# A full rewrite of a block-sparse attention plus Hyena-gate kernel: fp16 gate, wide exps, natural-layout PV, radix-2 DFT, merged work streams

## The chip, the cores and the metric

The kernel runs on one core of one Trainium2 chip. The metric is the time of one execution in device microseconds. Each kernel was run several times, in rounds that alternate with the kernel before on the same chip, and one execution was recorded by the hardware profiler (its span is a microsecond or two shorter than the time). A run that is over 1.5% above the fastest run of the same kernel is called slow and is left out of ratios. The engines are PE (matrix multiplication), PEld (PE's weight loads, which overlap its matmuls), DVE (vector engine), ACT (scalar engine), POOL and SP (which only issues transfers here). PSUM is the memory that PE's results go to; a program divides it into buffers.

## The reference, cut to what matters

```python
def _attn_ref(q, k, v):                       # 4 batches, 8 heads, 768 positions, head size 64
    k_rep = k.reshape(B, H, 12, 64, D).mean(axis=3)           # one mean key per block of 64
    gate_scores = einsum('bhsd,bhnd->bhsn', q, k_rep)         # then causal by blocks
    top_idx = argsort(gate_scores)[..., -3:]                  # the 3 best blocks, and the own block
    scores = scale * q @ k.T                                  # masked by blocks and causally
    return softmax(scores) @ v

def _moe_ref(x, w_proj, filter_fft, w_out):   # x: 4 x 768 x 512
    x1, x2, x3 = split(x @ w_proj, 3)
    x2_conv = irfft(rfft(x2) * rfft(filter_fft))              # along the 768 positions
    return (x1 * x2_conv * x3) @ w_out
```

## The kernel before: the parts that matter here

Attention runs head by head. Scores are computed transposed (keys on partitions) in pieces of 128 to 384 queries, each with its own exp. PV (the product of the exps with V) is also transposed: the stationary operand is V with 64 columns of ones beside it, so rows 64 to 127 of the result hold the softmax sum, 64 times over. Its reciprocal is made on ACT from a logarithm and an exponential.

```python
    ps_sc = ... bufs=3      # scores, and much else
    ps_ot = ... bufs=1      # the PV sum: one buffer
    ...
                    nc.tensor.matmul(sps, lhsT=augK[...], rhs=augQ[0:76, qs:qe], ...)
                    nc.scalar.activation(ex[:, 0:w], sps, AF.Exp, bias=bias_exp, scale=scale)
                    ...                                   # POOL: causal mask on diagonal pieces
                    nc.tensor.matmul(oT[:, qs - hs:qe - hs], lhsT=v_aug[:, kc, :], rhs=ex[:, 0:w], ...)
            # once per half of a head, 64 times in all:
            nc.scalar.activation(den[64:128, :], oT[64:128, :], AF.Ln, bias=0.0, scale=1.0)
            nc.scalar.activation(den[64:128, :], den[64:128, :], AF.Exp, bias=0.0, scale=-1.0)
            nc.vector.tensor_tensor(out=xT[...], in0=oT[0:64, :], in1=den[64:128, :], op=ALU.mult)
```

The gate is an fp32 matmul with the queries as the stationary operand and only 12 moving columns. The FFT of the Hyena part is a full real DFT by matmul: 2 x 3 groups of six 512-column matmuls forward, and six of 384 columns for each piece of the inverse. Hyena of a batch is added as low-priority pieces during the attention of the next batch.

The softmax here doesn't subtract the row's maximum and nothing guards it: scores larger than these inputs give would overflow.

Of the kernel before, what the change touches and what calls it, by code (L numbers as in the profile page):

```python
# [9 lines left out]
FP32 = mybir.dt.float32  # L11
# [7 lines left out]
def kernel(  # L19
# [10 lines left out]
    nc = tc.nc  # L30
# [3 lines left out]
    SC = S // P  # L34
    NBLK = S // 64
    Dm = H * D
    DC = Dm // P
    N3 = 3 * Dm
    F = 384
    FCH = S // P  # L40
    HALF = 384

    scale = 1.0 / math.sqrt(D)
    GBIG = 240.0
    EXPB = -GBIG * scale
    CBIG = 1.0e5
    BIG2 = 1.0e9
    TWO_PI = 2.0 * math.pi
    MAGIC = float(2 ** 23)

    fp = FP16

    const = ctx.enter_context(tc.tile_pool(name="const", bufs=1))
    hpool = ctx.enter_context(tc.tile_pool(name="hpool", bufs=3))
    aug = ctx.enter_context(tc.tile_pool(name="aug", bufs=5))
    augp = ctx.enter_context(tc.tile_pool(name="augp", bufs=5))
    qtfp = ctx.enter_context(tc.tile_pool(name="qtfp", bufs=3))
    expp = ctx.enter_context(tc.tile_pool(name="expp", bufs=8))
    small = ctx.enter_context(tc.tile_pool(name="small", bufs=6))
    xtp = ctx.enter_context(tc.tile_pool(name="xtp", bufs=2))  # L60
    p2 = ctx.enter_context(tc.tile_pool(name="p2", bufs=1))
    p2b = ctx.enter_context(tc.tile_pool(name="p2b", bufs=2))
    outp = ctx.enter_context(tc.tile_pool(name="outp", bufs=3))

    ps_trans = ctx.enter_context(tc.tile_pool(name="ps_trans", bufs=1, space=bass.MemoryType.PSUM))
    ps_sc = ctx.enter_context(tc.tile_pool(name="ps_sc", bufs=3, space=bass.MemoryType.PSUM))
    ps_ot = ctx.enter_context(tc.tile_pool(name="ps_ot", bufs=1, space=bass.MemoryType.PSUM))
    ps_ms = ctx.enter_context(tc.tile_pool(name="ps_ms", bufs=2, space=bass.MemoryType.PSUM))

    def tr_tile(name, shape, dtype=FP32):  # L70
        return ps_trans.tile(list(shape), dtype, name=name, tag="trans", padded_shape=[P, 1024])

    def sc_tile(name, shape=(P, 512), dtype=FP32):
        return ps_sc.tile(list(shape), dtype, name=name, tag="sc")

    def ot_tile(name, shape=(P, HALF), dtype=FP32):
        return ps_ot.tile(list(shape), dtype, name=name, tag="ot")

    def ms_tile(name, shape=(P, 512), dtype=FP32):
        return ps_ms.tile(list(shape), dtype, name=name, tag="ms")  # L80

    id_f32 = const.tile([P, P], FP32)
    make_identity(nc, id_f32)
    id_f16 = const.tile([P, P], fp)
    nc.gpsimd.tensor_copy(id_f16, id_f32)

    ebig = const.tile([P, S], fp)
    nc.gpsimd.memset(ebig[64:76, :], GBIG)
    nc.gpsimd.affine_select(
        out=ebig[64:76, :], in_=ebig[64:76, :], compare_op=ALU.is_ge,  # L90
        fill=0.0, base=0, pattern=[[1, S]], channel_multiplier=-64)
    nc.gpsimd.affine_select(
        out=ebig[64:76, :], in_=ebig[64:76, :], compare_op=ALU.is_ge,
        fill=0.0, base=63, pattern=[[-1, S]], channel_multiplier=64)

    ownb = const.tile([P, SC, NBLK], fp)
    nc.gpsimd.memset(ownb, 0.0)
    nc.gpsimd.affine_select(
        out=ownb[0:64], in_=ownb[0:64], compare_op=ALU.not_equal,
        fill=1.0, base=0, pattern=[[-2, SC], [1, NBLK]], channel_multiplier=0)  # L100
    nc.gpsimd.affine_select(
        out=ownb[64:128], in_=ownb[64:128], compare_op=ALU.not_equal,
        fill=1.0, base=-1, pattern=[[-2, SC], [1, NBLK]], channel_multiplier=0)

    eavg = const.tile([P, SC, NBLK], FP32)
    nc.gpsimd.memset(eavg, 0.0)
    nc.gpsimd.affine_select(
        out=eavg[0:64], in_=eavg[0:64], compare_op=ALU.not_equal,
        fill=1.0 / 64.0, base=0, pattern=[[-2, SC], [1, NBLK]], channel_multiplier=0)
    nc.gpsimd.affine_select(  # L110
        out=eavg[64:128], in_=eavg[64:128], compare_op=ALU.not_equal,
        fill=1.0 / 64.0, base=-1, pattern=[[-2, SC], [1, NBLK]], channel_multiplier=0)
    NW = P + NBLK
    ideav = const.tile([P, SC, NW], FP32)
    for c in range(SC):
        nc.gpsimd.tensor_copy(ideav[:, c, 0:P], id_f32)
        nc.gpsimd.tensor_copy(ideav[:, c, P:NW], eavg[:, c, :])

    e01f = const.tile([P, S], FP32)
    nc.gpsimd.memset(e01f[64:76, :], 1.0)  # L120
    nc.gpsimd.affine_select(
        out=e01f[64:76, :], in_=e01f[64:76, :], compare_op=ALU.is_ge,
        fill=0.0, base=0, pattern=[[1, S]], channel_multiplier=-64)
    nc.gpsimd.affine_select(
        out=e01f[64:76, :], in_=e01f[64:76, :], compare_op=ALU.is_ge,
        fill=0.0, base=63, pattern=[[-1, S]], channel_multiplier=64)
    cmat = const.tile([P, NBLK], FP32)
    nc.gpsimd.memset(cmat[64:76, :], 0.0)
    nc.gpsimd.affine_select(
        out=cmat[64:76, :], in_=cmat[64:76, :], compare_op=ALU.is_ge,  # L130
        fill=-CBIG, base=0, pattern=[[-1, NBLK]], channel_multiplier=1)

    tri01 = const.tile([P, P], fp)
    nc.gpsimd.memset(tri01, 1.0)
    nc.gpsimd.affine_select(
        out=tri01, in_=tri01, compare_op=ALU.is_ge,
        fill=0.0, base=0, pattern=[[1, P]], channel_multiplier=-1)

    bias_exp = const.tile([P, 1], FP32)
    nc.gpsimd.memset(bias_exp, EXPB)  # L140
    cr0 = const.tile([P, 1], FP32)
    nc.gpsimd.memset(cr0, 2.0 / S)
    nc.gpsimd.memset(cr0[0:1, :], 1.0 / S)
    cr0n = const.tile([P, 1], FP32)
    nc.gpsimd.memset(cr0n, -2.0 / S)
    nc.gpsimd.memset(cr0n[0:1, :], -1.0 / S)

    tvals = const.tile([1, S], fp)
    nc.gpsimd.iota(tvals, pattern=[[1, S]], base=0, channel_multiplier=0,
                   allow_small_or_imprecise_dtypes=True)  # L150
    fvals = const.tile([1, S], fp)
    nc.gpsimd.iota(fvals, pattern=[[0, 2], [1, F]], base=0, channel_multiplier=0,
                   allow_small_or_imprecise_dtypes=True)
    onesrow = const.tile([1, S], fp)
    nc.gpsimd.memset(onesrow, 1.0)
    offrow = const.tile([1, S], fp)
    nc.gpsimd.memset(offrow[:, 0:F], 192.0)
    nc.gpsimd.memset(offrow[:, F:S], 384.0)
    altrow = const.tile([1, S], fp)
    nc.gpsimd.iota(altrow, pattern=[[0, S // 2], [1, 2]], base=0, channel_multiplier=0,  # L160
                   allow_small_or_imprecise_dtypes=True)
    nc.gpsimd.tensor_scalar(altrow, in0=altrow, scalar1=-2.0, scalar2=1.0, op0=ALU.mult, op1=ALU.add)
    altcol = const.tile([P, 1], fp)
    acp = sc_tile("acp", (P, 1))
    nc.tensor.matmul(acp, lhsT=altrow[:, 0:P], rhs=onesrow[:, 0:1], start=True, stop=True)
    nc.vector.tensor_copy(altcol, acp)

    RT = const.tile([P, FCH, S], fp)
    R = const.tile([P, FCH, S], fp)

    def gen_dft_piece(dst_ap, rvals_ap, cvals_ap, off_ap, ncols):
        pr = sc_tile("dftp", (P, ncols))
        nc.tensor.matmul(pr, lhsT=rvals_ap, rhs=cvals_ap, start=True, stop=False)
        nc.tensor.matmul(pr, lhsT=onesrow[:, 0:P], rhs=off_ap, start=False, stop=True)
        ka = p2b.tile([P, 512], FP32, name="dft_ka", tag="dft_ka")
        nc.vector.tensor_scalar(ka[:, 0:ncols], in0=pr, scalar1=1.0 / S,
                                scalar2=MAGIC, op0=ALU.mult, op1=ALU.add)
        nc.vector.tensor_scalar(ka[:, 0:ncols], in0=ka[:, 0:ncols], scalar1=-MAGIC,
                                scalar2=-float(S), op0=ALU.add, op1=ALU.mult)
        nc.vector.tensor_add(pr, pr, ka[:, 0:ncols])  # L180
        nc.scalar.activation(dst_ap, pr, AF.Sin, bias=0.0, scale=TWO_PI / S)

    for tcn in range(FCH):
        rv = tvals[:, P * tcn:P * (tcn + 1)]
        gen_dft_piece(RT[:, tcn, 0:F], rv, fvals[:, 0:F], offrow[:, 0:F], F)
        gen_dft_piece(RT[:, tcn, F:S], rv, fvals[:, F:S], offrow[:, F:S], F)
    for rc in range(FCH):
        rv = fvals[:, P * rc:P * (rc + 1)]
        offsl = offrow[:, 0:F] if rc < 3 else offrow[:, F:S]
        gen_dft_piece(R[:, rc, 0:F], rv, tvals[:, 0:F], offsl, F)  # L190
        gen_dft_piece(R[:, rc, F:S], rv, tvals[:, F:S], offsl, F)

    wp = const.tile([P, DC, N3], fp)
    wo = const.tile([P, DC, Dm], fp)
    fil = const.tile([P, SC, Dm], fp)
    with tc.tile_pool(name="staging", bufs=2) as staging:
# [51 lines left out]
    def attention_prep(b, h):  # L248
# [45 lines left out]
        for c in range(SC):  # L294
            nc.vector.max(m8[:, c, :], gps[:, c, :])
# [200 lines left out]
```

## Time and profile before

The median is 678.2 us (678.15 to 682.07 in the first three runs).

| | PE | DVE | ACT | POOL |
|---|---|---|---|---|
| busy, us of a span of 684.2 | 510 | 263 | 443 | 135 |
| share | 75% | 38% | 65% | 20% |

The mean granted PE clock is 0.790 of full speed. The first lines below are from the profile page of the kernel before: busy time of each engine in all, and the granted clock in 40 equal slices of the span, in tenths of full speed.

```profile
PE 510.1 (75%) x2467; PEld 301.8 (44%) x2467; DVE 263.1 (38%) x675; ACT 443.3 (65%) x665; POOL 134.5 (20%) x327
PEclk9999766655688886985666888895577868898999
```

The next lines are the groups of instructions on ACT and two of PE (line, engine, operation, output<-input, shapes, count, then busy us and mean ns of one, then idle time before them and who ended it).

```profile
L325 ACT ACTIVATE ex<-sps,bias_exp 128x384 f16<-128x384 f32 x160 | 89.6, 580 | 21.2 <-PE sps L322 18.4
L334 ACT ACT_TABLE_LOAD x64 | 82.1, 1283 | 1.2
L325 ACT ACT_TABLE_LOAD x49 | 62.9, 1283 | 3.2 <-PE sps L322 2.4
L335 ACT ACT_TABLE_LOAD x16 | 20.5, 1283 | 0.3
L289 PE MATMUL gps<-krep,qTf 76*128 76x12 f32 x384 | 63.7, 303 | 1.2 <-DVE t_4507 L384 0.9 <-DVE t_3363 L384 0.3
```

130 table loads, by which ACT changes between functions (129 at these three lines, one more at the start), take 167 us. The Trainium skill, "ScalarE: Activation LUTs", section "What ACT_TABLE_LOAD costs", gives about 1283 ns for one; the trace agrees to the nanosecond. (The same sentence of it adds about 1380 ns of drain to every switch. That doesn't show in this trace: in the lines below, the next activation starts within 0.02 us of the load's end.) The timeline of ACT around 160 us (start, length, what):

```profile
163.21 1.28 ACT L334 ACT_TABLE_LOAD   x1
164.51 0.49 ACT L334 ACTIVATE den<-oT_1293 64x384 f32<-64x384 f32 x1
165.01 1.28 ACT L325 ACT_TABLE_LOAD   x1
166.31 0.58 ACT L325 ACTIVATE ex<-sps,bias_exp 128x384 f16<-128x384 f32 x1
166.91 0.52 ACT L335 ACTIVATE den<-den 64x384 f32<-64x384 f32 x1
```

The view of waits: PE waits for exps that would free a score buffer (engine, line, waited for: us in total, times, longest).

```profile
DVE xT L336 <- ACT den L335: 152.3, 58, 6.3
PE sps L322 <- ACT ex L325: 103.0, 71, 3.4
```

### The profile page before, as it was taken

Reading aid. Unit: us, or ns where it says so; the run is one execution under the profiler, and the core shown is the slowest. Engines: PE = TensorE matmul, PEld = TensorE weight load, DVE = VectorE, ACT = ScalarE, POOL = GpSimd, SP = SyncE. Lnnn points to the kernel's source line nnn. Section 1 sums busy time; section 2 is a strip of 40 time slices with the busy share of each in tenths; the row PEclk is TensorE's granted clock in tenths of the full one; section 3 lists DMA queues with packets and bytes.
Section 4 is the critical chain, followed back from the end, with each engine's and each line's share of the span. In section 5 each row is a group of like instructions: output and inputs, shape, how many; then the busy total and the mean of one; then the engine's idle time right before and its main releaser. Section 6 shows DMA issues by size and latency. Waiting matters only on the chain.

```text
span 684.2 us, 7602 instructions
## 1 busy us (share of the span) xinstructions
PE 510.1 (75%) x2467; PEld 301.8 (44%) x2467; DVE 263.1 (38%) x675; ACT 443.3 (65%) x665; POOL 134.5 (20%) x327
## 2 busy tenths in 40 slices
PE   0547877785788767969948867887966867858987
PEld 0212655562664545536714344444734343433343
DVE  3785323221344334423413333532322434431562
ACT  0134699999987898561199789663179899663302
POOL 9410011212111224110012133220011133200130
PEclk9999766655688886985666888895577868898999
DMA  7541222212323221400312121310210000001002
GB/s 253 142 104 39 58 52 56 53 44 61 74 42 64 57 57 44 106 13 13 93 55 60 43 55 22 71 25 21 67 60 24 7 9 0 1 0 55 38 1 92
DMA packets 88199, 36.46 MB, mean 53 GB/s; under 512 B 80480, under 2 KB 82912, under 8 KB 88160
## 3 DMA queue, kind: packets, MB, share of 16 engines
q1 hardware_dynamic: 84704, 29.69, 18.4%
q10 hardware_dynamic: 3456, 6.29, 2.4%
q8 instruction: 19, 0.31, 0.2%
q14 instruction: 20, 0.16, 0.1%
HBM read 24.64 MB, written 6.29 MB: 45 GB/s over the span
## 4 chain that ended last, share of the span: by engine, by line
PE 44%; ACT 34%; issue 11%; DVE 5%; POOL 4%; DMA 0%; POOLq 0%; SPq 0%; ACTq 0%
ACT ex L325 11%; ACT L334 8%; PE tp L268 6%; PE gps L289 6%; PE cv L398 5%; PE sps L322 4%; ACT den L334 3%; ACT den L335 3%; PE x2ps L355 3%; PE op L424 2%; PE x3p L409 2%; ACT L325 2%; PE x1p L404 2%; ACT L335 2%; ACT augQ L276 2%
## 5 line engine op out<-in xcount | busy, mean ns | idle before, releaser
L325 ACT ACTIVATE ex<-sps,bias_exp 128x384 f16<-128x384 f32 (+2 forms) x288 | 135.1, 508 | 63.6 <-PE sps L322 29.6
L322 PE MATMUL sps<-augQ,augK 76*128 76x384 f16 (+2 forms) x288 | 90.0, 349 | 107.6 <-ACT ex L325 103.0
L327 POOL TENSOR_SCALAR_AFFINE_SELECT ex<-ex 128x128 f16<-128x128 f16 x192 | 55.0, 292 | 439.5 <-ACT ex L325 436.8
L268 PEld LDWEIGHTS tp<-ideav,qk_nat 128*128 128x128 f32 x384 | 73.1, 254 | 54.3 <-issue 45.8
L268 PE MATMUL tp<-ideav,qk_nat 128*128 128x140 f32 x384 | 81.5, 360 | 20.4 <-DMA qk_nat<-in_k_dram 17.8
L334 ACT ACT_TABLE_LOAD x64 | 82.1, 1283 | 1.2
L289 PEld LDWEIGHTS gps<-krep,qTf 76*128 76x128 f32 x384 | 64.4, 254 | 18.8 <-issue 14.7
L325 ACT ACT_TABLE_LOAD x49 | 62.9, 1283 | 3.2 <-PE sps L322 2.4
L289 PE MATMUL gps<-krep,qTf 76*128 76x12 f32 x384 | 63.7, 303 | 1.2 <-DVE t_4507 L384 0.9
L322 PEld LDWEIGHTS <-augK 76*128 76x128 f16 x288 | 33.0, 120 | 61.4 <-issue 53.0
L330 PEld LDWEIGHTS <-v_aug 128*128 128x128 f16 x288 | 35.2, 128 | 53.2 <-issue 31.7
L427 ACT COPY osb<-op 128x512 f32<-128x512 f32 x24 | 13.7, 586 | 67.5 <-PE op L424 66.2
L276 ACT CAST augQ<-tp 64x768 f16<-64x768 f32 x32 | 25.2, 786 | 42.1 <-DVE qTf L274 41.9
L398 PE MATMUL cv<-R,Ysb 128*128 128x384 f16 x192 | 47.8, 363 | 5.6 <-POOL Ysb L383 2.6
L274 DVE COPY qTf<-tp 64x768 f32<-64x768 f32 x32 | 30.3, 947 | 31.9 <-PE tp L268 31.8
L355 PE MATMUL x2ps<-wp,xT 128*128 128x512 f16 x96 | 33.3, 485 | 2.5 <-ACT osb L427 1.6
L335 ACT ACTIVATE den<-den 64x384 f32<-64x384 f32 x64 | 33.2, 519 | 1.4
L304 DVE COPY augQ<-gmt 12x768 f16<-12x768 f16 x32 | 17.8, 555 | 39.8 <-PE gmt L301 39.6
L404 PE MATMUL x1p<-xT,wp 128*128 128x384 f16 x128 | 32.7, 358 | 0.1
L424 PE MATMUL op<-wo,yT 128*128 128x512 f16 x96 | 30.5, 427 | 2.0 <-DVE yT L416 2.0
L409 PE MATMUL x3p<-xT,wp 128*128 128x384 f16 x128 | 31.7, 344 | 0.0
L398 PEld LDWEIGHTS <-Ysb 128*128 128x128 f16 x192 | 20.2, 109 | 24.1 <-issue 11.6
(611 smaller groups left out, 697.0 us busy)
## 6 DMA issues: line engine op xcount, KB each, us to landing
qk_nat<-in_q_dram SPq DMA_DIRECT2D x32, 192.0 KB
qk_nat<-in_k_dram SPq DMA_DIRECT2D x32, 192.0 KB
v_nat<-in_v_dram SPq DMA_DIRECT2D x32, 192.0 KB
out_dram<-osb ACTq DMA_DIRECT2D x24, 256.0 KB
wst<-in_moe_w_proj_dram SPq DMA_DIRECT2D x4, 768.0 KB
qTf<-e01f SPq DMA_DIRECT2D x32, 36.0 KB
augK<-ebig SPq DMA_DIRECT2D x32, 18.0 KB
krep<-cmat SPq DMA_DIRECT2D x32, 0.6 KB
```

The source lines that it names most:

```text
L268: nc.tensor.matmul(tp[:, CS * c:CS * c + NW], lhsT=qk_nat[:, c, :, :], rhs=ideav[:, c, :], start=True, stop=True, skip_group_check=True)
L289: nc.tensor.matmul(gps[:, c, :], lhsT=qTf[0:76, P * c:P * (c + 1)], rhs=krep[0:76, :], start=True, stop=True)
L322: nc.tensor.matmul(sps, lhsT=augK[0:76, P * kc:P * (kc + 1)], rhs=augQ[0:76, qs:qe], start=True, stop=True)
L325: nc.scalar.activation(ex[:, 0:w], sps, AF.Exp, bias=bias_exp, scale=scale)
L327: nc.gpsimd.affine_select(out=ex[:, 0:P], in_=ex[:, 0:P], compare_op=ALU.is_ge, fill=0.0, base=0, pattern=[[1, P]], channel_multiplier=-1)
L334: nc.scalar.activation(den[64:128, :], oT[64:128, :], AF.Ln, bias=0.0, scale=1.0)
L335: nc.scalar.activation(den[64:128, :], den[64:128, :], AF.Exp, bias=0.0, scale=-1.0)
L355: nc.tensor.matmul(pp, lhsT=xT[:, dc, P * tcn:P * (tcn + 1)], rhs=wp[:, dc, Dm:2 * Dm], start=(dc == 0), stop=(dc == DC - 1))
L398: nc.tensor.matmul(cv, lhsT=Ysb[:, fc, P * dc:P * (dc + 1)], rhs=R[:, fc, hs:hs + HALF], start=(fc == 0), stop=False)
L404: nc.tensor.matmul(x1p, lhsT=wp[:, dc2, P * dc:P * (dc + 1)], rhs=xT[:, dc2, hs:hs + HALF], start=(dc2 == 0), stop=(dc2 == DC - 1))
L409: nc.tensor.matmul(x3p, lhsT=wp[:, dc2, 2 * Dm + P * dc:2 * Dm + P * (dc + 1)], rhs=xT[:, dc2, hs:hs + HALF], start=(dc2 == 0), stop=(dc2 ...
L424: nc.tensor.matmul(op, lhsT=yT[:, cc, P * scn:P * (scn + 1)], rhs=wo[:, cc, :], start=(cc == 0), stop=(cc == DC - 1))
```

## The change

The kernel is rewritten whole. Its parts are:

1. Gate: queries and mean keys are split into an fp16 value and an fp16 remainder, and four fp16 products replace the fp32 one. Mean keys (32 columns for a pair of heads) are the stationary operand, and four pairs use four column tiles of PE.
2. Scores are packed into three wide pieces a head (1024, 1024, 640 columns), each with one exp.
3. PV is in the natural layout: the exps are the stationary operand and V with one column of ones (65 columns) moves. Queries are on partitions, so the softmax sum is one number per partition and query chunk: 128x6. DVE takes its reciprocal.
4. The DFT works on even and odd halves (radix 2): half the forward columns, two thirds of the inverse ones.
5. Attention of a batch, Hyena of the batch before and preparation of the next batch are Python generators whose steps are merged by progress.

```diff
-            nc.scalar.activation(den[64:128, :], oT[64:128, :], AF.Ln, bias=0.0, scale=1.0)
-            nc.scalar.activation(den[64:128, :], den[64:128, :], AF.Exp, bias=0.0, scale=-1.0)
+        nc.vector.reciprocal(rec, pov[:, :, 64:65].rearrange("p c n -> p (c n)"))
 ...
-                    nc.scalar.activation(ex[:, 0:w], sps, AF.Exp, bias=bias_exp, scale=scale)
+        nc.scalar.activation(ex[:, 0:w], sp[:, 0:w], AF.Exp, scale=ESC)        # w = 1024, 1024, 640
 ...
-                    nc.tensor.matmul(oT[:, qs - hs:qe - hs], lhsT=v_aug[:, kc, :], rhs=ex[:, 0:w], ...)
+                nc.tensor.matmul(po[:, 65 * c:65 * c + 65], lhsT=exs[pi][:, col:col + P],
+                                 rhs=st["va"][:, kc, h, :], ...)
 ...
-            nc.tensor.matmul(gps[:, c, :], lhsT=qTf[0:76, P * c:P * (c + 1)], rhs=krep[0:76, :], ...)
+            for (wt, src) in ((kmh[i], q2h), (kml[i], q2h), (kmh[i], q2l), (kml[i], q2l)):
+                for j in range(j0, j0 + jn):
+                    nc.tensor.matmul(gt[32 * j:32 * j + 32, 0:w], lhsT=wt[:, j, :],
+                                     rhs=src[:, j, P + p0:P + p0 + w], ...)
 ...
+                streams = [Stream(attn_gen(st), T_ATT), Stream(hyena_gen(prev), T_HY)]
+                if nxt is not None:
+                    streams.append(Stream(prep_gen(nxt), T_PREP, 0.0, 0.9))
+            merge(streams)
 ... (V and weights by casting transfers on POOL's queue; masks by 12 extra rows of Qt; all else rewritten)
```

## The prediction

> **What bounds the kernel now.** No engine fills the span of 684 us (PE 75%, ACT 65%, DVE 38%, POOL 20%), but stages differ. From 100 to 280 us ACT is busy 163 of 180 us, and the waits view puts 103 us of PE's idle on exps that free score buffers: attention is bound by ACT. Of ACT's 443 us, 130 table loads of 1283 ns are 167 us; the log and exp that make the reciprocal are about 64. The first 80 us hold only 40 us of PE work. The last Hyena batch, from 635 us, runs at clock 1.00; elsewhere the clock falls (0.62 in 160 to 200 us, mean 0.79). The Trainium skill, "TensorE: Matmul & The Clock Gate", Part 1, says that the clock follows PE activity; this trace agrees.
>
> **What the change does, costed.**
> ACT: reciprocals go to DVE, so 3 table loads remain (-163 us) and log/exp go (-64). Exps become 64 of 1024 and 32 of 640 columns: from 366/472/580 ns at 128/256/384 (0.84 ns a column plus 259) about 1.1 and 0.8 us, 97 us for 143. Casts at 0.49 (384) and 0.59 us (512) are about 90. ACT falls from 443 to about 195 us.
> PE, at full clock (384 columns issue every 162 ns, 512 every 215 ns): scores 36 us (as before); PV 672 pairs of 65 columns at 55 to 60 ns (pairs of the mask transpose issue every 55 ns) 39; x1/x3 42; inverse DFT 21 for 36; forward DFT 13 to 18 for 36; x2 21; output 21; q/k transposes 25 to 45; gate about 10 for 46, if four column tiles run together (skill, "TensorEngine Tiling (Array Packing)", Key Properties: tiles run in parallel; no run yet shows it here); rest 20. Sum about 265 us, against 345 counted so for before.
> DVE: about 220 us (263 before), products 0.56 (384) and 0.69 us (512). POOL: 96 masks of about 0.4 us, 24 sums of 1.27, 16 products of about 1.9, and descriptor work for 34 casting DMAs: 110 to 180 us.
>
> **On the critical path.** ACT's 250 us lie nearly all on it, but PE is next: 265 us cannot be undercut. Stages: start about 22 us instead of some 85; batch 0 about 58; batches 1 and 2, three streams, 61 us of PE work each at about 0.8 (clock times activity) 77 each; batch 3 about 64; last Hyena alone about 38. With 14 us for coupling of in-order queues over four rotating PSUM buffers: 350 us.
>
> **Predicted:** 350 us, 8 in 10 between 305 and 400. Faster by over 2%: 0.98; within 2%: 0.01; slower: 0.01.
>
> **What would show each step right.** ACT_TABLE_LOAD x3; ACT about 195 us; exps near 1.1 us; PE the busiest engine, mean clock about 0.9; gate matmuls overlapping in fours; PV pairs at 55 to 60 ns; first exp before 30 us; about 38 us after the last exp; no single wait over 40 us in total, PE's waits spread over DVE and ACT readers of PSUM.
>
> **What would make it wrong.** PV pairs bound by weight loads (100 ns or more: +30 us). Gate matmuls running one after another (+12 us). POOL becoming the limit, since masks, products and casting DMAs share its queue and PV waits for masks. Four PSUM buffers, one held by PV for most of a head, stalling the merged order: PE would idle on DVE and ACT releases and its clock would fall to 0.7, giving 400 us or more. Better interleaving than I allow would give 305.

## The result, and the profile after

The kernel after takes 326.93 us (median of 4 runs, 326.72 to 327.18), against 680.14 us for the kernel before in the same rounds. The ratio is 0.4805, with a 95% interval of 0.4782 to 0.4828. Ratios here are the mean time of one kernel's fast runs over that of the other's fast runs in the same rounds, so they are not quite the ratio of the medians quoted.

The profile page of the kernel after, the lines that answer to those shown above:

```profile
PE 263.0 (81%) x2134; PEld 148.6 (46%) x2134; DVE 196.9 (61%) x644; ACT 175.3 (54%) x285; POOL 138.3 (43%) x202
PEclk9999998899978999999999999999999999999999
```

PE's busy time has halved, ACT's has fallen by 268 us, and the mean clock has risen from 0.790 to 0.979. The groups of instructions, with exps, PV, the fp32 transposes and the normalisation:

```profile
L389 ACT ACTIVATE ex<-sp 128x1024 f16<-128x1024 f32 x64 | 63.9, 1029 | 22.5 <-PE sp L385 22.0
L389 ACT ACTIVATE ex<-sp 128x640 f16<-128x640 f32 x32 | 22.8, 714 | 5.1 <-PE sp L385 4.8 <-POOL ex L391 0.2
L403 PE MATMUL po<-va,ex 128*128 128x65 f16 x672 | 36.0, 196 | 1.7 <-PE qp L248 1.5
L261 PE MATMUL kp<-id_91,kn 128*128 128x128 f32 x96 | 19.5, 327 | 6.3 <-DVE ms L345 3.4 <-DVE q2l L250 1.8 <-issue 0.4
L411 DVE RECIPROCAL rec<-po 128x6 f32<-128x6 f32 x32 | 6.1, 189 | 19.0 <-PE po L403 18.5 <-DVE prod L503 0.3
```

Three table loads are left. A mean of 196 ns for a PV matmul is its latency (from start to end), not its spacing. The timeline of PE gives the spacing: the first line below has nine matmuls in 0.44 us, and less the 0.19 us that the last one needs to finish, 8 intervals take 0.25 us, about 31 ns each. The other line is six in 0.34 us: (0.34 - 0.19) / 5 = 30 ns.

```profile
243.22 0.44 PE L403 MATMUL po<-va,ex 128*128 128x65 f16 x9
244.63 0.34 PE L403 MATMUL po<-va,ex 128*128 128x65 f16 x6
```

Busy times by stage (the view of windows: stretch, its length, busy us and instructions of PE, PEld, DVE, ACT, POOL, then clock, DMA share, GB/s). The stretches are the start, batch 0, the two batches with three streams, the batch with two, and the last Hyena.

```profile
0.00:40.00 40.00, 14.39 (x54) 7.75 (x54) 27.65 (x77) 11.94 (x20) 27.10 (x48) 1.00 1.41 201
40.00:112.00 72.00, 54.38 (x483) 35.21 (x482) 39.94 (x203) 40.45 (x66) 16.74 (x33) 0.91 0.82 129
112.00:175.00 63.00, 56.67 (x504) 32.20 (x503) 44.11 (x140) 39.04 (x65) 28.44 (x41) 1.00 0.43 94
175.00:237.00 62.00, 57.75 (x512) 33.33 (x511) 42.51 (x140) 39.27 (x66) 27.99 (x39) 1.00 0.46 89
237.00:280.00 43.00, 42.69 (x371) 23.11 (x369) 24.57 (x49) 28.68 (x42) 22.03 (x31) 1.00 0.06 20
280.00:325.00 45.00, 37.13 (x220) 17.02 (x219) 18.13 (x35) 15.95 (x31) 16.06 (x12) 1.00 0.19 71
```

In the steady stages (112 to 280 us) PE is busy 90 to 99% at full clock. The first 40 us hold only 14 us of PE work. There the transfers are dense (201 GB/s), and DVE stands still for one of them. The timeline of DVE (in brackets: idle before it, and what ended it):

```profile
32.82 0.69 DVE L198 TENSOR_TENSOR x2o<-f_747,f_748 128x512 f16<-128x512 f32 x1 [5.17 <-DMA f_748<-in_moe_filter_fft_dram]
33.43 0.47 DVE L345 COPY ms<-mt 24x640 f16<-24x640 f16 x1
```

The copy `ms`, which the mask of the first scores needs, stands behind a subtraction that waits for the filter. The first exp starts at 39.7 us (77.8 us in the kernel before).

### The profile page after: what moved, and what is told of

It is laid out like the page before. It is cut to its first block, busy times and chain, and to the rows that moved or that the text cites. A ratio compares the mean times of both kernels' runs of the same rounds, so it can differ in the third digit from the quotient of the medians.

```text
span 325.2 us, 6030 instructions
## 1 busy us (share of the span) xinstructions
PE 263.0 (81%) x2134; PEld 148.6 (46%) x2134; DVE 196.9 (61%) x644; ACT 175.3 (54%) x285; POOL 138.3 (43%) x202
## 4 chain that ended last, share of the span: by engine, by line
PE 53%; DVE 14%; DMA 11%; ACT 8%; POOL 6%; issue 4%; SPq 2%; POOLq 1%; ACTq 0%; DVEq 0%
PE x13p L495 9%; PE sp L385 8%; PE x2p L464 5%; PE cv L511 5%; PE po L403 5%; ACT ex L389 5%; DMA f_748<-in_moe_filter_fft_dram 4%; PE op L524 3%; PE kp L261 3%; PE qp L248 3%; PE gt L289 3%; POOL yT L519 2%; DVE ks L263 2%; PE xp L423 2%; DMA qn<-in_q_dram 2%
## 5 line engine op out<-in xcount | busy, mean ns | idle before, releaser
L389 ACT ACTIVATE ex<-sp 128x1024 f16<-128x1024 f32 (+1 forms) x96 | 85.9, 924 | 27.6 <-PE sp L385 26.8
L391 POOL TENSOR_SCALAR_AFFINE_SELECT ex<-ex 128x256 f16<-128x256 f16 x96 | 39.8, 417 | 114.4 <-ACT ex L389 114.4
L495 PE MATMUL x13p<-xT,wp 128*128 128x384 f16 x256 | 49.0, 326 | 1.7 <-ACT x_2170 L501 0.6
L519 POOL TENSOR_TENSOR yT<-prod,sd 128x768 f16<-128x768 f32 x16 | 29.0, 1810 | 28.2 <-DVE sd L518 25.3
L403 PEld LDWEIGHTS <-ex 128*128 128x128 f16 x672 | 30.8, 99 | 15.4 <-issue 7.6
L403 PE MATMUL po<-va,ex 128*128 128x65 f16 x672 | 36.0, 196 | 1.7 <-PE qp L248 1.5
L495 PEld LDWEIGHTS <-wp 128*128 128x128 f16 x256 | 23.6, 98 | 17.5 <-issue 4.9
L250 DVE SCALAR_TENSOR_TENSOR q2l<-qp,q2h 128x384 f16<-128x384 f32 x32 | 17.2, 550 | 23.0 <-ACT q2h L249 22.6
L511 PE MATMUL cv<-G,Y 128*128 128x384 f16 (+1 forms) x128 | 28.9, 327 | 1.4 <-POOL Y L484 0.9
L249 ACT ACTIVATE q2h<-qp 128x384 f16<-128x384 f32 x32 | 15.7, 496 | 23.0 <-PE qp L248 22.6
L237 POOL DMA_DIRECT2D va<-in_v_dram x32 | 26.9, 861 | 0.0
L261 PE MATMUL kp<-id_91,kn 128*128 128x128 f32 x96 | 19.5, 327 | 6.3 <-DVE ms L345 3.4
```

What stands on the lines that cost most here:

```text
L237: nc.gpsimd.dma_start(st["va"][:, :, 2 * j + t, 0:D], v_r[st["b"], :, :, 2 * j + t, :])
L261: nc.tensor.transpose(kp[:, P * c:P * (c + 1)], kn[:, HC * hf + c, :, :], id32)
L389: nc.scalar.activation(ex[:, 0:w], sp[:, 0:w], AF.Exp, scale=ESC)
L391: nc.gpsimd.affine_select(out=dv, in_=dv, compare_op=ALU.is_ge, fill=0.0, base=0, pattern=[[0, 2], [1, P]], channel_multiplier=-1)
L403: nc.tensor.matmul(po[:, 65 * c:65 * c + 65], lhsT=exs[pi][:, col:col + P], rhs=st["va"][:, kc, h, :], start=(kc == 0), stop=(kc == c), sk ...
L495: nc.tensor.matmul(xp[:, 0:HS], lhsT=wp[:, d2, base + P * dc:base + P * (dc + 1)], rhs=xT[:, d2, hs:hs + HS], start=(d2 == 0), stop=(d2 == ...
```

## The experiments

Twelve kernels ran. Times are medians. Edits to the kernel after are compared with its 326.9 us; edits to the kernel before with the kernel before in the same rounds. Times of different rounds come from different chips, on which the medians of the kernel before differ by 0.6% (680.1 to 684.3 us), so differences of the new kernel's variants of a microsecond or two say nothing.

### 1. The old kernel with one part of the change: DVE's reciprocal

```diff
-            nc.scalar.activation(den[64:128, :], oT[64:128, :], AF.Ln, bias=0.0, scale=1.0)
-            nc.scalar.activation(den[64:128, :], den[64:128, :], AF.Exp, bias=0.0, scale=-1.0)
+            nc.vector.reciprocal(den[64:128, :], oT[64:128, :])
```

> The old kernel with one part of the change alone: the reciprocal of the softmax sum by one DVE RECIPROCAL (64x384, 64 of them) in place of ACT's log and exp. This also removes about 128 of the 130 table loads of 1283 ns. Theory (ACT bounds the old attention): ACT busy falls from 443 to about 212 us, PE becomes the busiest, and the time falls by 100 to 190 us, to between 490 and 580. Rival (the serial chain of transposes, gate and DMA hops per head bounds it, ACT only fills it): less than 60 us saved. If DVE's reciprocal is slow per column (the new kernel shows 189 ns for 6 columns, no run shows 384), DVE may take the place of ACT and hide the gain; DVE's busy time tells.

Measured: 649.6 us against 681.7; ratio 0.9536 (0.9486 to 0.9585). Only 32 us were saved, although ACT's busy time fell from 443 to 214 us. On busy time alone the rival seems to win. But the third possibility named in the expectation had occurred, as the groups of DVE in this run show:

```profile
L334 DVE RECIPROCAL den<-oT 64x384 f32<-64x384 f32 x64 | 163.8, 2560 | 53.4 <-PE oT L330 52.9
L335 DVE TENSOR_TENSOR xT<-oT,den 64x384 f16<-64x384 f32 x64 | 35.1, 548 | 1.8
```

A reciprocal of 384 columns takes 2560 ns, almost five times a product of the same shape. By the two sizes seen it costs (2560 - 189) / (384 - 6) = 6.3 ns a column (an estimate, since the two also differ in partitions). The hop from the PV sum to its reciprocal was at least 3.57 us on ACT (two loads, 487 and 519 ns), and mostly 4.2 us, since an exp of the scores stands between, as in the timeline above; it is now 2.56 us on DVE. So this run doesn't tell what an idle ACT is worth. It does show that the wait of PE for exps was not by itself what bound the kernel: that wait fell from 103 to 27 us, and the time by 32. Nor is any engine full now: these are the wait in this run, and the busy times from 100 to 280 us (the view of windows again):

```profile
PE sps L322 <- ACT ex L325: 26.9, 55, 1.4
100.00:280.00 180.00, 141.24 (x703) 96.34 (x702) 121.50 (x212) 69.69 (x135) 37.64 (x102) 0.67 0.26 58
```

ACT is busy 70 of these 180 us (163 before), DVE 122 and PE 141, at a clock of 0.67.

### 2. The old kernel with almost no work in that hop (wrong on purpose)

```diff
-            nc.scalar.activation(den[64:128, :], oT[64:128, :], AF.Ln, bias=0.0, scale=1.0)
-            nc.scalar.activation(den[64:128, :], den[64:128, :], AF.Exp, bias=0.0, scale=-1.0)
+            nc.scalar.activation(den[64:128, :], oT[64:128, :], AF.Copy, bias=0.0, scale=1.0e-5)
```

> The old kernel with log and exp of the softmax sum replaced by one scaled ACT copy: a wrong result on purpose, with no table load and one hop of about 0.5 us in place of about 3.5 us (487 and 519 ns and two loads of 1283 ns). The run with DVE's reciprocal kept a hop of 2.56 us and saved only 32 us. Theory (the old kernel waits, 64 times, for the one PSUM buffer of the PV sum to be normalised: the length of that hop counts, ACT's busy time does not): 64 x 2.5 = 160 us fewer, 540 to 580 us. Rival A (ACT's busy time counted and DVE took its place): also large, so this run tells only from rival B. Rival B (PE at its lowered clock and the preparation of heads bound it): 620 us or more.

Measured: the two fast runs took 509.3 and 515.3 us (two slow ones 519 and 520); ratio 0.748 (0.742 to 0.754), which is 173 us of the 685.0 us mean of the kernel before. It is below the expected 540 to 580. (Its wrong values go on into the Hyena part; that values leave the times alone is assumed here.) ACT is busy 242 us here, more than in experiment 1, and yet the kernel is some 137 us faster. So in experiment 1 it was not ACT's busy time that counted, but the slow reciprocal in its place. Whether that reciprocal costs by its length in the chain or by DVE's time as a whole (rival A), this run can't tell, as its expectation says; that DVE was busy only 122 of 180 us in experiment 1 speaks for the length. The profile of this run is of a slow execution, so the following is read for its kind only. The same 2467 matmuls are busy 440 us at clock 0.914, against 510 us at 0.790, and PE's wait for exps has nearly gone (the first line is from the page, the second from the view of waits):

```profile
PE 439.9 (85%) x2467; PEld 265.5 (51%) x2467; DVE 261.7 (50%) x675; ACT 241.5 (47%) x473; POOL 133.8 (26%) x327
PE sps L322 <- ACT ex L325: 11.7, 21, 1.2
```

Between these two spans (684.2 and 518.7 us), 70 us of 165 are PE doing the same work faster, and 95 us are idle that went. The skill's "TensorE: Matmul & The Clock Gate", Part 1, says that PE's clock is set by how busy PE has lately been; these two runs agree, with 0.790 at 75% busy and 0.914 at 85%. The busy share of a long stretch doesn't give the clock, though: in the kernel before it is 0.63 from 120 to 160 us with PE 78% busy, and 0.84 from 600 to 620 us with PE 65% busy. The hop seems to have mattered twice: it stood ahead of exps, and PE's pauses behind it cost clock. How much is due to the single PV buffer and how much to exps that stand behind the loads is not separated by these runs. The direct waits speak for the second: in the view of waits of the kernel before, PE waits for exps for 103 us, but for the PV buffer (`oT <- DVE xT`) only 7.2 us in all, so the theory's 64 waits for that buffer do not show there.

### 3. The new kernel with log and exp put back into the chain

```diff
-        nc.vector.reciprocal(rec, pov[:, :, 64:65].rearrange("p c n -> p (c n)"))
+        nc.scalar.activation(rec, pov[:, :, 64:65].rearrange("p c n -> p (c n)"), AF.Ln)
+        nc.scalar.activation(rec, rec, AF.Exp, scale=-1.0)
```

> The new kernel with the reciprocal put back on ACT as log and exp of 128x6, which brings about 64 or more table loads back. ACT busy rises from 175 to about 270 us, below the span of 325. Theory (the new kernel is bound by PE, ACT has slack): +5 to +40 us, well under the ACT time added. Rival (ACT still lies on the critical path): +80 us or more, the whole of the ACT time added.

Measured: 415.1 us, so +88 us. The theory falls: ACT rose by 92 us, to 267 us of a span of 413 us, 65% busy, and nearly all of it showed in the time. The trace has 67 table loads. DVE's product, and all that stands behind it in DVE's order, waits for ACT:

```profile
DVE xn L416 <- ACT rec L412: 78.1, 24, 13.1
```

PE's 2134 matmuls are busy 295 us at clock 0.883, for 263 us at 0.979. An engine that is busy only 65% of the span can thus be critical. The next three runs ask whether the crossing to ACT, ACT's time, or the place of the loads does this.

### 4. Only the crossing: two ACT copies in the chain

```diff
         nc.vector.reciprocal(rec, ...)
+        reca = qkT.tile([P, NQ], FP32, name="reca", tag="reca")
+        nc.scalar.copy(reca, rec)
+        nc.scalar.copy(reca, reca)
+        rec = reca
```

> The new kernel, DVE reciprocal kept, then two ACT copies of 128x6 in the chain before the DVE product: the same two hops through ACT as the run with log and exp, without table loads. Result right. ACT busy +12 us. Theory (what cost 88 us with log and exp is the time that the normalise chain holds DVE's in-order queue and the PV buffer, of which 82 us are table loads): +8 to +30 us. Rival (the crossing between engines itself is what costs): +60 us or more.

Measured: 330.4 us, +3.4 us. The 95% intervals of the ratios to the kernel before overlap (0.4804 to 0.4846 here, 0.4782 to 0.4828 for the kernel after), so even this is not clear of noise. Two copies on ACT per head cost little, less than the theory allowed. The table loads are needed for the 88 us.

### 5. Only the loads: log and exp that nobody waits for

```diff
         nc.vector.reciprocal(rec, ...)
+        junk = qkT.tile([P, NQ], FP32, name="junk", tag="junk")
+        nc.scalar.activation(junk, rec, AF.Ln)
+        nc.scalar.activation(junk, junk, AF.Exp, scale=-1.0)
```

> The new kernel, DVE reciprocal kept and used, and log and exp of 128x6 added on ACT once per head with nobody waiting for their result: about 64 more table loads, ACT busy about 267 us as in the run with log and exp in the chain. Theory (the place in the chain is what costs): +5 to +40 us, less than half of the 88. Rival (ACT's time itself is critical, wherever it stands): +75 us or more.

Measured: 369.6 us, +43 us, with 67 table loads and ACT busy 264 us, as in experiment 3. This lies between theory and rival: the loads (with their log and exp) cost half of the 88 us even when nothing depends on them. What ACT has to do next, exps and casts, stands behind them in its order. (The skill, "PSUM — Partial Sum Buffer", section "Engine vs sequencer instructions", states that ACT, DVE and POOL run strictly in order; these traces agree: the copy `ms` above stood behind a wait of 5.17 us.) The other 45 us, the difference to experiment 3, come from the loads' place in the chain. Waits on ACT's casts show where part of the first half goes, in this run's view of waits. In the kernel after, the first of these waits is 22.6 us and the second 5.0; PE's wait for exps has also grown, from 3.1 to 12.3 us, and the clock has fallen to 0.949.

```profile
DVE q2l L250 <- ACT q2h L249: 29.3, 13, 12.0
DVE ks L263 <- ACT k L262: 19.0, 13, 2.7
```

### 6. Twice as many exps

```diff
-        nc.scalar.activation(ex[:, 0:w], sp[:, 0:w], AF.Exp, scale=ESC)
+        for c0, c1 in ((0, 512), (512, w)):
+            nc.scalar.activation(ex[:, c0:c1], sp[:, c0:c1], AF.Exp, scale=ESC)
```

> The new kernel with each wide exp cut in two at the PSUM bank border (512 and 512 or 512 and 128 columns): 96 more ACT instructions of some 190 ns fixed cost, about +18 us of ACT time, PE and DVE untouched. Theory (ACT has slack): under +4 us. Rival (ACT on the critical path): +15 us or more.

Measured: 326.7 us, no difference. But the test was weaker than planned: ACT's busy time rose by 5.1 us only (175.3 to 180.4). By length, the exps are as planned: 615 and 309 ns in place of 1029 and 714, which adds up to 19.6 us more. But all save 5.1 us of it overlaps other activations, about 151 ns for each of the 96 (an estimate from these numbers). The skill's "ScalarE: Activation LUTs", section "What ACT_TABLE_LOAD costs", says that back-to-back activations overlap by about 93 ns; that accounts for 8.9 of the 14.5 us, and the rest is not explained. In the new kernel, packing two banks into one exp is therefore worth nothing by itself. It says nothing about 18 us more of ACT work.

### 7. The gate's column tiles, in another order

```diff
-            for (wt, src) in ((kmh[i], q2h), (kml[i], q2h), (kmh[i], q2l), (kml[i], q2l)):
-                for j in range(j0, j0 + jn):
+            for j in range(j0, j0 + jn):
+                for n_, (wt, src) in enumerate(((kmh[i], q2h), (kml[i], q2h), (kmh[i], q2l), (kml[i], q2l))):
```

> The new kernel, gate matmuls of batches 1 to 3 reordered so that the four terms of one column tile follow each other, in place of four column tiles in turn. Same instructions, same work. If column tiles run in parallel only when neighbours differ, each group of 16 takes 16 x 160 ns (384 columns) and 16 x 107 ns (256) in place of about 1.2 us and 0.8: +2.2 us of PE a batch. Theory (tiles run together, PE is the limit): +4 to +8 us. Rival A (tiles never ran in parallel): spacing unchanged and 0. Rival B (parallel, but PE's time there is not critical): spacing four times as long and less than 2 us.

Measured: 326.0 us (324.9 to 328.5), no difference. The theory and rival B had assumed that the order in the text decides. It does not; and rival A, that tiles never ran in parallel, is refuted by the traces. Here is PE's timeline in the kernel after, 16 gate matmuls of 256 columns, grouped by their operands:

```profile
146.63 0.29 PE L289 MATMUL gt<-q2h,kmh_110 128*32 128x256 f16 x4
146.75 0.28 PE L289 MATMUL gt<-q2h,kml_111 128*32 128x256 f16 x4
146.86 0.28 PE L289 MATMUL gt<-q2l,kmh_110 128*32 128x256 f16 x4
146.97 0.28 PE L289 MATMUL gt<-q2l,kml_111 128*32 128x256 f16 x4
```

And in this run, where the instruction stream has the four products of one tile, then the four of the next:

```profile
148.09 0.32 PE L289 MATMUL gt<-q2h,kmh 128*32 128x256 f16 x4
148.21 0.31 PE L289 MATMUL gt<-q2h,kml 128*32 128x256 f16 x4
148.32 0.31 PE L289 MATMUL gt<-q2l,kmh 128*32 128x256 f16 x4
148.43 0.31 PE L289 MATMUL gt<-q2l,kml 128*32 128x256 f16 x4
```

Four tiles start their first product within 40 ns (the lines group four matmuls of 0.28 us into 0.32), and each next product about 110 ns later. By the profiler's start times, the first product of the fourth tile, the 13th in the stream, starts before the second in the stream. So the tiles do run in parallel (the skill, "TensorEngine Tiling (Array Packing)", section "Key Properties", says so, and this trace agrees), and each tile goes on by itself. The cost of a gate without column tiles was not measured by this run.

### 8. The DFT matmuls doubled

```diff
-            for t in range(HC):
+            for u in range(2 * HC):
+                t = u % HC
 ...
+                terms = terms + terms          # inverse: 8 matmuls for 4; scales divided by 8
```

> The new kernel with every DFT matmul issued twice (forward, filter, inverse), scales divided by 8 so that the result stays right: the column count of a DFT without the radix-2 split, in the same schedule. It adds about 40 us of PE work at full clock (forward 15.6, filter 3.9, inverse 20.8) and nothing to the other engines. Theory (PE bounds batches 1 to 3 and the tail): +30 to +40 us. Rival (waits on PSUM readers and coupling of the in-order queues bound it, the PE has room): +15 us or less.

Measured: 361.8 us, +34.9 us, as the theory has it. 40 us of PE work (an estimate from 384 columns in 162 ns and 512 in 215 ns) cost 35 us: PE is the limit in most of the kernel. By the starts of the first exps it is so by stages, too: batches 1 to 3 and the last Hyena each take 7 to 10 us longer, for some 9 us of work added to each, while batch 0, where the filter's matmuls fall, takes no longer (71.0 us for 71.9).

Read the other way, this is an upper bound for what radix 2 is worth here. The expectation calls it the column count of a DFT without the split, which holds for the forward part only: the inverse of the kernel before has six matmuls a piece (and one of a single row for the last frequency), not the eight of this run. So 30 to 35 us of PE work would come back rather than 40 (an estimate from the same two figures).

### 9. The merge of the streams undone

```diff
-                streams = [Stream(attn_gen(st), T_ATT), Stream(hyena_gen(prev), T_HY)]
+                Stream(hyena_gen(prev), T_HY).drain()
+                Stream(attn_gen(st), T_ATT).drain()
+                streams = []                   # then the preparation of the next batch alone
```

> The new kernel with the merge of the streams undone for batches 1 to 3: the program text runs Hyena of the batch before, then attention, then the preparation of the next batch, each to its end. The work is the same. Theory (interleaving is what keeps PE busy at clock 1.00): PE waits for exps in attention, for evacuations in Hyena; a batch takes 75 to 95 us for 63, the total +35 to +90, clock below 0.95. Rival (the scheduler that orders the instructions fills gaps from later text by itself): within 3% of the new kernel.

Measured: 388.5 us, +61.6 us; clock 0.906, and PE busy 286 us for the same 2134 matmuls. From first exp to first exp, batches 1 and 2 take 95 and 89 us for 60 and 63. The theory holds; the scheduler's own filling does not replace the merge.

### 10. Three PSUM buffers for four

The edit is `bufs=3` in the pool of single-bank PSUM tiles.

> The new kernel with three single-bank PSUM buffers in place of four. The prediction named these buffers as the main danger and put 14 us of coupling on them. Theory (four suffice, PE waits little for them: its largest wait in the new trace is 10 us): three cost +5 to +20 us. Rival A (buffers are not near the limit at all): under +2 us. Rival B (buffers are the limit now): +30 us or more, and a fifth would be worth as much again.

Measured: 330.7 us, +3.8 us, a little under the range of the theory, and again with overlapping intervals of the ratios (0.4815 to 0.4853 for 0.4782 to 0.4828). PSUM buffers are not near being the limit.

### 11. The wait at the start removed

```diff
-            nc.vector.tensor_tensor(fo[:, t, :], f0, f1, op=ALU.subtract)
+            nc.gpsimd.tensor_tensor(fo[:, t, :], f0, f1, op=ALU.subtract)
```

> The new kernel with the three filter subtractions moved from DVE to POOL. In the trace DVE stands 5.2 us at 27.5 to 32.8 us on the load of the last filter piece, and the copy of the first gate mask, which the first scores need, stands behind it. Theory (this in-order wait delays the start): first exp at about 34 us for 39.7, and 3 to 6 us saved in all. Rival (the start is bound by the loads of q and k themselves, or batch 0 catches up later): less than 1 us.

Measured: 326.3 us. The first exp starts at 34.4 us for 39.7, as expected, but the first exp of batch 1 only at 109.2 for 111.6, and 0.6 us of the median is left. The rival is right about the total. In the profiled run batch 0 gives back 2.9 of the 5.3 us, and batch 1 another 1.0.

### 12. A version that starts faster

```diff
-            nc.vector.tensor_tensor(fo[:, t, :], f0, f1, op=ALU.subtract)
+            nc.gpsimd.tensor_tensor(fo[:, t, :], f0, f1, op=ALU.subtract)
-                rest = Stream(rest_pairs(), 18.0, 0.0, 0.6)
+                rest = Stream(rest_pairs(), 18.0, 0.0, 0.4)
-                    nc.gpsimd.tensor_mul(yT[:, dc, :], prod, sd)
+                    (nc.vector if tail["on"] else nc.gpsimd).tensor_mul(yT[:, dc, :], prod, sd)
```

> An attempt at a faster version of the new kernel: filter subtractions on POOL (first exp 5 us earlier, as shown), the preparation of pairs 1 to 3 of batch 0 pulled ahead of attention (end of its stream 0.4 in place of 0.6), and in the last Hyena the product on DVE (about 1 us) in place of POOL (1810 ns). Theory (batch 0, 36 to 109 us, is paced by the chain of pair preparations, about 14.5 us for each pair, with PE busy only 54 of 73 us): 4 to 12 us fewer. Rival (batch 0 is held by loads, and moving work does not help): within 2 us of the new kernel.

Measured: 321.4 us (319.8 to 322.4), a correct result, 5.5 us or 1.7% under the kernel after by medians; ratio to the kernel before 0.4691 (0.4671 to 0.4711), below the interval of the kernel after. It is the fastest version. Since the two ran in different rounds, it is a small gain well beyond the spread of either kernel rather than a measured one of two decimals. Its first exp of batch 1 is at 105.9 us, for 111.6 in the kernel after and 109.2 in experiment 11. So the whole gain is there before batch 1. Against experiment 11, pulling the pair preparations ahead keeps batch 0 from giving the early start back (it takes 71.6 us for 74.8), and the last Hyena is 0.9 us shorter.

## Why the prediction was right, and where its terms were off

The predicted time was 350 us with a range of 305 to 400; the measured 327 us lie inside, 7% below. The sum came out near partly by luck, because errors of both signs cancelled. The stages, from the starts of the first exps of the batches (39.7, 111.6, 171.4 and 234.3 us) and the start of the last exp (279.5 us):

| stage | predicted us | measured us |
|---|---|---|
| start | 22 | 39.7 |
| batch 0 | 58 | 71.9 |
| batch 1 | 77 | 59.8 |
| batch 2 | 77 | 62.9 |
| batch 3 | 64 | 45.2 |
| last Hyena, after the last exp | 38 | 45.7 |
| coupling of in-order queues | 14 | within the stages |
| sum | 350 | 325.2 |

- "ACT's 250 us lie nearly all on it": right in size, loose in its reason. Taking log and exp off the old kernel gives 173 us (experiment 2), but halving ACT's load with a 2.56 us reciprocal in the same place gives 32 us (experiment 1). These runs point to the hop from PV's sum to its reciprocal, and the exps behind its loads, as what lay on the path, not ACT's total; they don't fully exclude that ACT's total counted and that DVE's reciprocals took its place. The change cures it by two of its parts together: the natural layout makes the sum 128x6 in place of 64x384, and only at that size is DVE's reciprocal short (189 ns). The prediction costed the two separately and did not see that one needs the other.
- ACT "about 195 us" and 3 loads: 175 us and 3 loads. Exps "about 1.1 and 0.8 us": 1029 and 714 ns. The 259 ns of fixed cost were read from exps with a bias operand, which the new ones lack; (1029 - 714) / 384 gives 0.82 ns a column, and about 189 ns fixed. That the operand makes the difference was not tested.
- "PV pairs at 55 to 60 ns": 30 to 31 ns, so 672 pairs are about 20 us, not 39. This is the term of PE's sum that was most mis-sized. The transposes of q and k are 192 single instructions, not two a product as the fp32 products of before. They follow each other about 109 ns apart in the trace, so they are about 21 us, below "25 to 45".
- "265 us cannot be undercut": the busy figure of 263 us is near by chance, because busy time includes latencies. Corrected for PV and the transposes, the sum at full clock is about 230 us (an estimate).
- "0.8 (clock times activity)" for the steady stages: with PV's excess of about 5 us a batch, it made batches 1 to 3 50 us too long in all, the largest error. PE is busy 90 to 99% there at clock 1.00. Experiment 9 shows what holds it there: without the merge the clock is 0.906 and batches 1 and 2 take 95 and 89 us.
- Start and batch 0: 32 us too low together. The start has dense transfers (201 GB/s) and waits for one of them; batch 0, with PE busy 54 of 72 us, seems to be paced by preparing its pairs, which experiment 12 shows for some 3 us only. "First exp before 30 us" was missed by 10 us. Removing one wait of 5 us gained nothing by itself; with the preparations also moved ahead, about 5 us were gained (experiments 11 and 12).
- "Four PSUM buffers ... stalling": named as a danger; taking one more away costs 3.8 us. POOL was within its range (138 us) and did not become the limit.
- DVE "about 220 us": 197 us. "Mean clock about 0.9": 0.979. "About 38 us after the last exp": 45.7 us.
- "No single wait over 40 us in total": false by the letter, since POOL waits 114.4 us for exps, but POOL has that time to spare. No wait of PE's own is over 10 us, and its largest are:

```profile
PE mt L342 <- DVE nm L337: 9.4, 4, 5.2
PE gn L302 <- DVE kb L145: 5.1, 1, 5.1
```

The parts do not add up to the 353 us saved, because each part's worth depends on the others. Undone alone in the new kernel, they are worth 88 us (the reciprocal on ACT), 62 us (merging) and at most 35 us (radix 2, by doubling). The wide exps cut in two cost nothing (experiment 6). The fp32 gate and the transposed PV were not put back, so their own share stays open.

## What to carry to other kernels

Count for an engine not only its busy time but what stands in its order ahead of work that others wait for: 82 us of table loads on a half-idle ACT cost 43 us where nobody needed them and 88 us where the chain did. A layout that shrinks an awkward operation to a few columns can be worth more than moving that operation to another engine. And when pauses of PE go, PE's remaining work may run faster too: here the mean granted clock went from 0.79 to 0.98.

## What the Trainium skill lacked or had wrong

- "TensorE: Matmul & The Clock Gate", Part 3 ("strict FIFO, no reordering" of matmul starts), and "PSUM — Partial Sum Buffer", section "Engine vs sequencer instructions" (matmuls start in program order): not so across column tiles. In experiment 7 the 13th matmul of the stream started before the 2nd; four tiles each kept their own order, about 110 ns apart at 256 columns.
- "TensorE: Matmul & The Clock Gate", section "Back-to-back issue gap", gives about 81 ns for a sustained pair of weight load and matmul at 128 columns, and calls its formula for a single matmul, N/2.4 + 2.5 ns, too low at small N because it leaves the weight load out. Here it isn't: with 128x128 fp16 weights and 65 moving columns the pairs follow each other every 30 to 31 ns (the formula gives 29.6), and the 128-column fp16 transposes of L423, each with a weight load, about every 56 ns.
- No page that was consulted gives DVE's cost of a reciprocal per column ("VectorE: DVE Perf Modes", section "First, the fixed hardware budget", names an iterative divide with a repeat count of 8). The runs show 2560 ns for 64x384 and 189 ns for 128x6, from which 6.3 ns a column are estimated.
- "ScalarE: Activation LUTs", section "Table sets: the hidden batching unit", says that log followed by exp costs one load since one set has both. With the exps of the scores beside them, the kernels here paid 130 loads for 64 such pairs, and 67 for 32. In the kernel before, 16 of the loads stand at the reciprocal's own exp (L335), with no exp of the scores since its log, so even a log directly followed by its exp was charged two loads. Why the sets were chosen so is not shown.
